# Attention's maxima one to two units ahead of the weights, and unread products around unit 0

## The chip, the cores and the metric

The kernel runs on one core of a Trainium2 chip. A core has five engines with an instruction queue each, and each queue runs in order: PE (TensorE, matrix products into the accumulator memory PSUM), DVE (VectorE), ACT (ScalarE), POOL (GpSimd) and SP (SyncE, which only issues DMAs here). ACT and POOL issue some DMAs too. PEld is PE's loading of the stationary operand. The metric is the device time of one execution in microseconds; lower is better.

## The reference

The input is one sequence `x` of 2048 rows and 448 columns. The output is a gated mix, `g * a + (1 - g) * b`, with `g` the sigmoid of `x` times a vector. `a` is a long convolution along the sequence (its kernel K comes out of a state space model, and both are multiplied in the frequency domain). `b` is attention with a memory:

```python
q = (x @ wq) ... reshape(B, H, N, L, Dh)      # 16 heads of 28, 4 segments of 512 rows; k and v alike
for s in range(N):
    qs, ks, vs = q[:, :, s], k[:, :, s], v[:, :, s]
    logits = jnp.einsum("bhqd,bhkd->bhqk", qs, ks) * scale + mask
    p = _softmax(logits, axis=-1)
    a_dot = jnp.einsum("bhqk,bhkd->bhqd", p, vs)
    ...                                       # a_mem: what the memory of earlier segments gives
    o = g * a_mem + (1.0 - g) * a_dot
...
return o @ wo
```

Inside a segment the mask is causal. The softmax needs the largest logit of each row.

## The kernel before, in words

Up to about 484 us the kernel computes K, transforms `x`, and projects queries, keys and values, which it keeps in device memory. Then `second_half` (L1187) runs, and the change lies wholly in it.

**Units and steps.** Attention is cut into 16 units: unit `i` is segment `i // 4` and one group of four heads. Each piece of work is a Python generator, and `step` (L1193) issues its next part. So the order of PE's instructions is written out by hand in the loops of `second_half`: `k.mm` and `k.tr` (L1351 to L1355) are kept in program order. The other queues are ordered by a planner that follows the readiness it expects; it runs when the kernel is built.

**Maxima, `maxima(i)`, L954 to L987.** Six steps (`MSTEPS`) multiply queries by keys once, in low precision, and take each row's largest logit on DVE (L974, results in `mx`). The steps differ in width: in the first two each product has 512 columns, in the next two 384 and 128, in the last two 256. A seventh step does nothing. The eighth transposes `mx` on PE (L982), copies it with the sign turned on ACT and DVE (L984, L985, both out of the same PSUM bank `ps_m`, of which there is one), and writes it with a DMA from POOL (L986) into a spare row of the unit's queries `qu`. That row meets a row of ones of the keys, so that the products of the weights come out less their maximum.

**Weights, `weigh(i)`, L989 to L1016.** Six steps (`STEPS`) of the same widths in the same order multiply keys by queries, three times for precision, and apply the exponential on ACT (L1005, result in `PT`); POOL then zeroes what the mask hides (L1016). They read all of `qu`, the spare row too, and so wait for L986's DMA to land. Maxima take the heads in the other order, so that a step of maxima and the step of weights behind it lie on other row groups of the array.

**Values, `values(i)`, L1018 to L1037**, multiply `PT` by V. **`seg_end(s)`, L1128**, follows each segment: `norm` (L1074) gathers the sums of the rows by four DMAs from POOL (L1080), inverts them on DVE and sends them through device memory (`inverse`, L1039; its DMAs `RD` and `r`, L1049 and L1050, from POOL too), then products, scalings, the projection by `wo`, and `recall` of the memory for the next segment. `skip` (L1098) has a product on POOL (L1103, `xt`). `divide` (L1140) does the last segment's scaling group by group on PE and DVE, at the places in `DIVIDE`.

**Other work in the rounds.** `cv` is the convolution in the frequency domain (`convolve`, L562; `gk`, `gu`, `pr` in the names), stepped in units 1 to 12. `last` and `join` (L646, L651) end it in units 14 and 15. `turn_over(n)` (L1204) issues `n` products of 512 columns on the whole array, whose result nobody reads (`ps_pv<-wz`).

**The order around the change.** `transform_k` ("K's first step", eight rounds) runs with the steps of unit 0's maxima between its own, and its last two rounds with the first two steps of unit 1's maxima. Four more steps of unit 1's maxima follow, each behind three unread products. Then unit by unit there are six rounds. In each round of unit `i` before the change there come one step of the maxima of unit `i + 2` (`ahead`), one step of the weights of unit `i`, then other work; in rounds 0 and 1 the last two steps of the maxima of unit `i + 1` (`behind`), the transposes among them. PSUM's three large banks `ps_a` serve maxima, weights and convolution by turns. Queries and keys have four buffers each, and `load(i + 3)` is issued at the start of unit `i` from SP.

Of the kernel before, what the change touches and what calls it, by code (L numbers as in the profile page):

```python
# [459 lines left out]
class Feed:  # L460
# [9 lines left out]
    def step(self):  # L470
        tag = next(self.steps, None)
        self.count += 1
        self.done, self.held = tag is None, tag == "pe"
        cost = tag if isinstance(tag, float) else 0.0
        self.ends = cost < 0
        return abs(cost)
# [58 lines left out]
def transform_k(nc, k, fp):  # L535


    k2 = k.kb.rearrange("p b q -> p (b q)")
    gkv = k.GK.rearrange("k r n d -> (k r) n d")
    for i in range(8):  # L540
        gs = fp.tile([128, 4, 4, 112], F32, tag="gs", name="gs", bufs=4)
        pts = [k.ps("a") for jj in range(2)]
        for b in range(2):
            o = (32 * b + 4 * i) * 112
            for j in range(4):
                r = slice(32 * j, 32 * j + 32)
                k.mm(
                    pts[j // 2][:, j % 2, :448], k.s1k[r, b], k2[r, o : o + 448],
                    start=(b == 0), stop=(b == 1), tile_position=(32 * j, 0),
                )  # L550
        for jj in range(2):
            to = gs[:, :, 2 * jj : 2 * jj + 2].rearrange("p n j q -> p j n q")
            pt = pts[jj][:, :, :448].rearrange("p j (n q) -> p j n q", n=4)
            if jj == 0:
                nc.scalar.activation(to, pt, AF.Copy)
            else:
                nc.vector.tensor_copy(to, pt)
        k.mark(k.dma(gkv[:, 4 * i : 4 * i + 4], gs.rearrange("p n j q -> p n (j q)")))
        yield
# [71 lines left out]
def finish(nc, k, fp):  # L631

    bv = k.BB.rearrange("k r (h w) d -> (k r) h w d", h=2)
    ov = k.out.rearrange("(n h w) d -> h n w d", h=2, w=16)
    tv = k.TB.rearrange("(n h w) d -> h n w d", h=2, w=16)
    yv = k.YD.rearrange("(n h w) d -> h n w d", h=2, w=16)
    bts, rest = {}, {}  # L640

    def load(wc):
        bts[wc] = fp.tile([128, 2, 2, D], F32, tag="bt", name="bt", bufs=5)
        k.dma(bts[wc], bv[:, :, 2 * wc : 2 * wc + 2])

    def join(wc):  # L646
        rest[wc] = fp.tile([128, 2, D], F32, tag="rest", name="rest", bufs=6)
        for h in range(2):
            k.dma(rest[wc][64 * h : 64 * h + 64], tv[h, :, 2 * wc : 2 * wc + 2])

    def last(wc):  # L651
        ws = slice(2 * wc, 2 * wc + 2)
        py = k.ps("a")
        for w in range(2):
            for h in range(2):
                k.mm(
                    py[64 * h : 64 * h + 64, w, :D], k.fc, bts[wc][:, h, w],
                    start=True, stop=True, tile_position=(0, 64 * h),
                )
        yo = rest.pop(wc)  # L660
        for w in range(2):
            i = 2 * wc + w
            nc.vector.scalar_tensor_tensor(yo[:, w], py[:, w, :D], k.gt2[:, i : i + 1], yo[:, w], ALU.mult, ALU.add)
        for h in range(2):
            k.dma(yv[h, :, ws], yo[64 * h + 48 : 64 * h + 64])
        for h in range(2):
            k.dma(ov[h, :48, ws], yo[64 * h : 64 * h + 48])

    return load, join, last
# [517 lines left out]
def second_half(nc, k, ap, tp, fp, fin):  # L1187

    none = object()

    def step(g):  # L1193
        return next(g, none) is not none

    nothing = iter(())
    attend(nc, k, ap)
    k.load(0)


    wz = ap.tile([128, SEG], BF16, name="wz")
    nc.gpsimd.memset(wz, 1.0)

    def turn_over(n):  # L1204
        pt = k.ps("pv")
        for _ in range(n):
            k.mm(pt, wz[:, :128], wz, start=True, stop=True)

    first = transform_k(nc, k, tp)
    ms = {i: k.maxima(i) for i in range(16)}  # L1210
    for r in range(8):
        step(first)
        if r == 1:
            k.load(1)
        for _ in range((0, 1, 2, 1, 2, 1, 1, 0)[r]):
            step(ms[0])
        if r >= 6:
            step(ms[1])

    pm = k.ps("m")  # L1220
    k.tr(pm[:16, :128], k.gt, k.ident)
    g16 = ap.tile([16, 128], F32, name="g16")
    nc.vector.tensor_copy(g16, pm[:16, :128])
    k.dma(k.GD.rearrange("(i p) -> i p", p=128), g16)
    k.gt2 = ap.tile([128, 16], F32, name="gt2")
    for h in range(2):
        k.dma(k.gt2[64 * h : 64 * h + 64], k.GD.rearrange("(n h w) -> h n w", h=2, w=16)[h])
    fp = fp()
    cv = convolve(nc, k, fp)
    step(cv)  # L1230
    k.load(2)
    vals = k.values(0)
    step(vals)
    for r in range(4):
        turn_over(3)
        step(ms[1])
    ends = []
    acc = 0.0
    n = 0
    for i in range(16):  # L1240
        k.load(i + 3)
        ahead = ms.get(i + 2, nothing)
        behind = ms.get(i + 1, nothing)
        w = k.weigh(i)
        for r in range(6):
            if r in WARM:
                turn_over(WARM[r])
            step(ahead)
            step(w)
            if r == 0:  # L1250
                step(behind)
            if r == 1:
                if i > 0:
                    step(vals)
                step(behind)
                if i % 4 == 0 and i > 0:
                    ends.append(k.seg_end(i // 4 - 1))
            if r != 1 or i == 13:
                for _ in range(2 if i == 13 else 1):
                    while ends and not step(ends[0]):  # L1260
                        ends.pop(0)
            if (i, r) in DIVIDE:
                k.divide(DIVIDE[i, r])
            if 1 <= i <= 12:
                acc += RATIO
                while acc >= 1.0:
                    acc -= 1.0
                    step(cv)
            if i == 11 and r == 2:
                k.skip_last()  # L1270
            if i == 13 and r < 5:
                load_b(r)
            if i == 14 and r >= 2 or i == 15 and r < 4:
                last(n)
                turn_over(1)
                if n < 2:
                    join(n + 6)
                if n < 3:
                    load_b(n + 5)
                n += 1  # L1280
        step(w)
        if i == 1:
            k.load_wo()
        if i > 0:
            vals = k.values(i)
            step(vals)
        if i == 12:
            for _ in cv:
                pass
            load_b, join, last = finish(nc, k, fin())  # L1290
        if i == 13:
            for wc in range(6):
                join(wc)
    for e in ends:
        for _ in e:
            pass
    k.last_end(step, vals)
# [1 line left out]

RATIO = 1.15  # L1300
WARM = {3: 1, 4: 3, 5: 3}
DIVIDE = {(14, 2): 0, (14, 5): 1, (15, 3): 2}

# [1 line left out]
def gated_mix(ctx, tc, k):  # L1307
# [231 lines left out]
    with ExitStack() as st:  # L1539
        psum_pool(  # L1540
            st,
            {"m": ([128, 512], 1), "a": ([128, 2, 512], 3), "pv": ([128, 512], 1)},
        )
        ap = pool(st, "ap", "right")
        k.mk = ap.tile([128, 512], F32, name="mk")
        nc.sync.dma_start(k.mk, k.c_mk)
        k.dbc = ap.tile([128, D], F32, name="dbc")
        tp, cs = ExitStack(), ExitStack()

        def fourier():  # L1550
            tp.close()
            kst.close()
            return pool(cs, "fp")

        def final():
            cs.close()
            return pool(st, "fin")

        second_half(nc, k, ap, pool(tp, "tp"), fourier, final)
# [34 lines left out]
```

## Time and profile before

| | |
|---|---|
| time, median of 3 runs | 895.89 us (895.46 to 905.81) |
| the profiled execution: its time, its span | 897.03 us, 895.3 us |
| busy: PE, DVE, ACT, POOL | 86%, 67%, 60%, 19% of the span |
| mean granted clock of PE | 0.93 |
| first weights of unit 0, of unit 1, of unit 15 | 518.2, 533.1, 855.2 us |
| instructions | 18968 |

The span runs from the first to the last instruction that the profiler recorded; the execution's own time is 1.7 us longer. A line of a timeline has the start, the duration in us, the engine, the line of the kernel, the operation, the names of what is written and read (`out<-in`), the shape and a count; in brackets stands how long the engine was idle before it and what ended that. A line of the waits has who waited for whom, the total in us, how often, and the longest. A line that cuts the time into stretches has each engine's busy time with its instructions, then PE's granted clock as a share of full speed, the share of the DMA engines' time, and GB/s. Ends of PE's products are modelled, and a wait for several things is put down to the last one.

### The profile page before, as it was taken

To read this page: it belongs to the slowest core of one execution; us is meant where nothing else is said; L and a number is where in the kernel's file an instruction comes from. 1 tells how busy PE (TensorE), PEld (TensorE's weight loads), DVE (VectorE), ACT (ScalarE), POOL (GpSimd) and SP (SyncE) were. 2 spreads that over 40 slices of the span, in tenths; PEclk is the share of its full clock that TensorE was granted. 3 is DMA by queue.
4 is the path that set the end of the run, shared out by engine and by line. 5 is a ranking of instruction groups with operands and counts; after the bars stand their busy time and mean duration, and the time that the engine had idled before them with its cause. 6 is when DMAs were issued, how large, how long until landed. Compare 5 with 4: busy or idle time off the path is not lost.

```text
span 895.3 us, 18968 instructions
## 1 busy us (share of the span) xinstructions
PE 765.6 (86%) x7573; PEld 413.3 (46%) x7573; DVE 602.6 (67%) x1162; ACT 536.8 (60%) x636; POOL 172.7 (19%) x217
## 2 busy tenths in 40 slices
PE   1688597799887998898997989989998999788997
PEld 1365364465544664455653344434443444334433
DVE  7986187758867767688666866656575736665564
ACT  4876388878978788878885235554454434332220
POOL 5222200110011001110110012132313122333110
PEclk9996799999988999969999969999999999989799
DMA  8258662334334334333255995576556565455773
GB/s 240 83 137 270 208 208 62 97 114 140 122 101 137 123 107 130 127 105 111 100 194 204 333 339 177 182 237 212 176 197 202 175 212 193 152 191 205 197 239 101
DMA packets 88290, 153.11 MB, mean 171 GB/s; under 512 B 20626, under 2 KB 57162, under 8 KB 88154
## 3 DMA queue, kind: packets, MB, share of 16 engines
q1 hardware_dynamic: 79130, 140.83, 48.2%
q10 hardware_dynamic: 7424, 9.18, 3.0%
q0 software_dynamic: 1648, 1.89, 0.7%
q8 instruction: 60, 0.98, 0.5%
q14 instruction: 28, 0.23, 0.1%
HBM read 90.87 MB, written 60.63 MB: 169 GB/s over the span
## 4 chain that ended last, share of the span: by engine, by line
PE 57%; DVE 14%; ACT 13%; DMA 7%; issue 5%; POOL 1%; SPq 1%; ACTq 0%; DVEq 0%; POOLq 0%
PE ps_m L1352 22%; PE ps_a L1352 17%; PE ps_pv L1352 7%; PE ps_arg L1352 6%; PE ps_k L1352 4%; ACT cs L1317 4%; DVE jk L974 3%; PE ps_m L1355 2%; DMA dn<-pvs 2%; DVE Y L397 2%; DMA WD<-wsp 2%; ACT L1317 1%; DVE X L393 1%; DVE Y L398 1%; DVE pin_f L211 1%
## 5 line engine op out<-in xcount | busy, mean ns | idle before, releaser
L1005 ACT ACTIVATE PT<-ps_a 128x1024 f32<-128x1024 f32 (+1 forms) x96 | 84.5, 881 | 120.0 <-PE ps_a L1352 114.9
L974 DVE CUSTOM_DVE_ANT_0 jk<-ps_a,mk 128x512 f32<-128x512 f32 (+3 forms) x256 | 125.0, 488 | 43.9 <-PE ps_a L1352 36.6
L359 POOL TENSOR_TENSOR EX<-EX,cab 128x1024 f32<-128x1024 f32 x28 | 54.0, 1929 | 344.2 <-ACT EX L1317 317.4
L1317 ACT ACTIVATE cs<-ps_arg 128x1024 f32<-128x1024 f32 x111 | 107.3, 1019 | 15.7 <-PE ps_arg L1352 13.6
L1352 PE MATMUL ps_m<-xh,w 112*128 112x512 f32 x256 | 95.0, 424 | 10.9 <-DMA w<-WD 9.1
L1352 PE MATMUL ps_a<-qu,ku 32*128 32x512 f32 (+3 forms) x768 | 90.2, 356 | 1.8 <-DVE mx L974 1.1
L1352 PE MATMUL ps_k<-Y,X 128*32 128x64 f32 x3584 | 70.2, 238 | 22.1 <-DVE Y L398 22.1
L393 DVE TENSOR_TENSOR X<-EX,cs 128x1024 f32<-128x1024 f32 x56 | 69.8, 1247 | 26.1 <-ACT cs L1317 23.6
L1352 PEld LDWEIGHTS ps_k<-Y,X 128*32 128x32 f32 x3584 | 60.5, 121 | 51.4 <-DVE Y L398 35.7
L1016 POOL TENSOR_SCALAR_AFFINE_SELECT PT<-PT 128x256 f32<-128x256 f32 (+1 forms) x96 | 47.4, 496 | 173.9 <-ACT PT L1005 173.7
L397 DVE TENSOR_TENSOR Y<-EY,cs 128x1024 f32<-128x1024 f32 x56 | 70.1, 1252 | 0.0
L1352 PEld LDWEIGHTS ps_a<-qu,ku 32*128 32x128 f32 x768 | 62.7, 195 | 10.5 <-issue 3.2
L399 DVE SCALAR_TENSOR_TENSOR Y<-EY,cs 128x512 f32<-128x512 f32 x56 | 40.8, 728 | 38.5 <-ACT cs L1317 37.5
L1352 PEld LDWEIGHTS ps_m<-xh,w 112*128 112x128 f32 x256 | 50.0, 195 | 35.9 <-issue 19.3
L1317 ACT ACTIVATE cs<-cs,bhp 128x1024 f32<-128x1024 f32 x56 | 64.4, 1150 | 1.8
L1317 ACT ACTIVATE EY<-ps_arg 128x1024 f32<-128x1024 f32 x52 | 52.7, 1039 | 10.0 <-PE ps_arg L1352 10.0
L1352 PE MATMUL ps_a<-ku,qu 32*128 32x512 f32 (+3 forms) x256 | 46.6, 397 | 10.8 <-DVE mx L974 7.2
L1352 PE MATMUL ps_m<-xl,w 112*128 112x512 f32 x128 | 51.8, 404 | 0.0
L1352 PEld LDWEIGHTS ps_a<-ku,qu 32*128 32x128 f32 x256 | 22.5, 191 | 58.6 <-DVE mx L974 29.6
L1352 PEld LDWEIGHTS <-lh 64*128 64x128 bf16 x392 | 21.4, 96 | 59.0 <-issue 46.7
L1352 PE MATMUL ps_arg<-ct,lh 64*128 64x512 bf16 x224 | 42.7, 396 | 4.5 <-ACT cs L1317 3.6
L1352 PE MATMUL ps_arg<-ce,lh 64*128 64x512 bf16 x168 | 37.7, 430 | 9.3 <-ACT EY L1317 4.5
(214 smaller groups left out, 1402.8 us busy)
## 6 DMA issues: line engine op xcount, KB each, us to landing
w<-WD SPq DMA_DIRECT2D x32, 448.0 KB, 3.8
qu<-QD SPq DMA_DIRECT2D x16, 512.0 KB, 6.4
ku<-KD SPq DMA_DIRECT2D x16, 512.0 KB, 4.8
GU<-gs SPq DMA_DIRECT2D x32, 224.0 KB, 3.4
GK<-gs SPq DMA_DIRECT2D x8, 896.0 KB, 3.6
gk<-GK SPq DMA_DIRECT2D x32, 224.0 KB, 4.4
gu<-GU SPq DMA_DIRECT2D x32, 224.0 KB, 3.5
BB<-bs ACTq DMA_DIRECT2D x16, 448.0 KB
```

Of the source, the lines that this page charges most:

```text
L211: x = op(*args, **kw)
L359: nc.gpsimd.tensor_tensor(o, o, cab, ALU.mult)
L393: v.tensor_tensor(X, ex, t[:, :, 0], ALU.mult)
L397: v.tensor_tensor(Y[:, :, :, :32], lo, y[:, :, :, ::-1], ALU.mult)
L398: v.tensor_tensor(Y[:, 0, :, 32:], ey[:, :, 32:], y[:, 0], ALU.mult)
L399: v.scalar_tensor_tensor(Y[:, 1, :, 32:], ey[:, :, 32:], -1.0, y[:, 1], ALU.mult, ALU.mult)
L974: v.tensor_tensor_reduce(junk[:, :n], pt[:, x, o : o + n], k.mk[:, SEG - n :], 1.0, -3e38, ALU.add, ALU.max, mx[:, 3 - t, h : h + 1],)
L1005: nc.scalar.activation(PT[:, 2 * hp : 2 * hp + 2, 512 * b : 512 * b + n], pt[:, :, :n], AF.Exp, scale=SCALE)
L1016: nc.gpsimd.affine_select(sl, sl, pat, ALU.is_ge, 0.0, base=0, channel_multiplier=-1)
L1317: x = op(*args, **kw)
L1352: tc.keep_in_program_order(nc.tensor.matmul(*args, **kw))
L1355: tc.keep_in_program_order(nc.tensor.transpose(*args))
```

## The change

The four steps of unit 1's maxima between K's first step and unit 0 are left out, with their twelve unread products. In the rounds, maxima run in another order: rounds 0 to 3 of unit `i` take the third to the sixth step of unit `i + 1`, rounds 4 and 5 the first two steps of unit `i + 2`. The seventh and eighth step of unit `i + 1` (the transposes, the copies and the DMA of L986) come in round 4, behind that round's weights. In unit 0 ten unread products stand in front of round 0's maxima and three in front of each later round's; in the other units they stay as they were (one, three and three in rounds 3, 4 and 5). The end of a segment makes no step in round 4 where it made none in round 1, so that its first step comes in round 1. Two of the three places of `divide` in the last units move.

```diff
     step(vals)
-    for r in range(4):
-        turn_over(3)
-        step(ms[1])
     ends = []
...
         w = k.weigh(i)
         for r in range(6):
-            if r in WARM:
+            if i == 0:
+                turn_over(3 if r else 10)
+            elif r in WARM:
                 turn_over(WARM[r])
-            step(ahead)
+            step(behind if r < 4 else ahead)
             step(w)
-            if r == 0:
+            if r == 4:
+                step(behind)
                 step(behind)
             if r == 1:
                 if i > 0:
                     step(vals)
-                step(behind)
                 if i % 4 == 0 and i > 0:
                     ends.append(k.seg_end(i // 4 - 1))
-            if r != 1 or i == 13:
+            if r != 4 or i == 13:
...
-DIVIDE = {(14, 2): 0, (14, 5): 1, (15, 3): 2}
+DIVIDE = {(14, 4): 0, (15, 0): 1, (15, 3): 2}
```

## The prediction

> **What bounds the kernel now.** I read the page first, for the engines' shares and the chain that ended last.
>
> ```profile
> span 895.3 us, 18968 instructions
> PE 765.6 (86%) x7573; PEld 413.3 (46%) x7573; DVE 602.6 (67%) x1162; ACT 536.8 (60%) x636; POOL 172.7 (19%) x217
> PE 57%; DVE 14%; ACT 13%; DMA 7%; issue 5%; POOL 1%; SPq 1%; ACTq 0%; DVEq 0%; POOLq 0%
> ```
>
> TensorE (PE) is the bound on average. The edit touches only the stretch from K's first step to the end, so I cut that stretch: first the front of the units, then units 0 and 1. The columns are the busy time of each engine, the granted clock, the DMA share and GB/s.
>
> ```profile
> 509.70:518.10 8.40, 5.11 (x27) 2.09 (x28) 7.55 (x30) 0.11 (x1) 0.00 (x0) 1.00 0.93 331
> 518.10:533.10 15.00, 14.26 (x79) 8.35 (x79) 8.63 (x35) 5.79 (x7) 2.91 (x7) 0.55 0.90 331
> 533.10:548.80 15.70, 15.70 (x133) 7.42 (x133) 10.57 (x35) 9.01 (x11) 3.59 (x8) 1.00 0.43 142
> ```
>
> Three different limits stand side by side. In front of unit 0 PE is idle for 3.3 of 8.4 us. Unit 0 runs its 15 us at a clock of 0.55, with 79 matmuls where unit 1 has 133. Unit 1 has PE busy for the whole of its 15.7 us at full clock: there, whatever PE must wait for is added to the time. PE's waits from unit 0 on, and the timeline of PE in front of unit 0, say what the idle time is:
>
> ```profile
> PE ps_a L1352 <- DVE mx L974: 8.2, 10, 2.5
> PE ps_a L1352 <- DVE pr L599: 7.0, 8, 4.4
> PE ps_a L1352 <- DMA ku<-KD: 3.3, 1, 3.3
> ```
>
> ```profile
> 510.30 0.81 PE L1352 MATMUL ps_pv<-wz 128*128 128x512 bf16 x3
> 518.12 0.79 PE L1352 MATMUL ps_a<-ku,qu 32*128 32x512 f32 x2 [3.26 <-DMA ku<-KD]
> ```
>
> PE's queue is in order. The maxima of unit 2 stand in front of the first weights of unit 0, and they wait for unit 2's keys until 518.12; the weights of unit 0 need none of them.
>
> **The chain that the change moves.** A unit's maxima must come back as rows of `qu` before its weights: four transposes, a copy on ACT, one on DVE, a DMA from POOL, its landing. Unit 1's pass, in the timeline of all engines, and two answers on the landing of that DMA (first in the window 500 to 535, two of them; then all 16):
>
> ```profile
> 522.02 1.01 PE L1355 MATMUL ps_m<-ident,mx 128*4 128x128 f32 x4
> 523.07 0.59 ACT L984 ACTIVATE mn<-ps_m 4x512 fp32r<-4x512 f32 x1
> 523.69 0.68 DVE L985 SCALAR_TENSOR_TENSOR mn<-ps_m,mn 4x512 fp32r<-4x512 f32 x1 [1.72 <-ACT mn L984]
> 524.66 0.58 POOL L986 DMA_DIRECT2D qu<-mn  x1 [1.03 <-DVE mn L985]
> ```
>
> ```profile
> DMA to landing us min/median/max: 3.2/4.2/5.2
> DMA to landing us min/median/max: 2.2/3.2/5.3
> ```
>
> From the first transpose to POOL's issue it is 2.64 us here, of which the transposes take 1.01 at half clock. On PE at full clock they take about half, so 2.2 us. With the landing the chain takes 4.4 us at best, 5.4 us at the median landing of 3.2, and 7.5 at the longest. Before, it starts in round 1 and has five rounds. After, it starts in round 4, behind that round's weights, and is needed at the first product of the next unit: one round and a bit. The wait itself is not new, but its cover is.
>
> **Part 1: the front.** Four maxima steps and 12 unread products leave the stretch before unit 0. Ten products stand in round 0 instead: 10 x 0.27 (0.81 for three) from 510.30 ends at 513.0. Unit 1's next maxima have their data, and they share PE with weights on other row groups, as the rows of the next fence show, so the first weights start near 513.1 and not at 518.2. The landing of unit 0's own maxima doesn't hold them; POOL's timeline has its DMA out early, and 508.65 + 3.2 is 511.9:
>
> ```profile
> 508.65 0.61 POOL L986 DMA_DIRECT2D qu<-mn  x1 [25.92 <-DVE mn L985]
> ```
>
> That is -5.1 us at the start of unit 0. The products are all on PE's path; in rounds 1 to 5 there are 15 of them, 4.1 us, where seven stood. Unit 0 at full clock, by rows of unit 1 in part 2 (weights 0.96 us for 512 columns, in four rounds, and 0.62 for 256, in two): 5.1 for the weights, 4.1 for the products, 0.6 for the transposes, and an estimated 1.8 for waits on DVE: 11.6 us instead of 14.9. So PE would stand at the first weights of unit 1 at 524.7, where it stood at 533.1.
>
> It won't go on there. The transposes fall near 522.5 (524.7 less one round of products and weights, 1.5, and the transposes, 0.6). DMA is full there:
>
> ```profile
> 525.00:530.00 5.00, 4.93 (x28) 3.11 (x27) 2.80 (x15) 1.93 (x2) 1.04 (x3) 0.50 1.03 385
> ```
>
> so I take the long landing of this window: 2.2 + 5.2 = 7.4, unit 1's weights at 529.9, a gain of 3.2 us (bounds: chain 4.4, gain 6.2; chain 7.8 with cold transposes, gain 2.8).
>
> **The clock after that wait.** PE then is idle from 524.7 to 529.9. What follows idle time of that length is seen in unit 11, behind the longest wait of PE for `pr`, 4.4 us:
>
> ```profile
> 766.00:768.00 2.00, 0.80 (x2) 0.29 (x4) 2.00 (x6) 0.00 (x0) 0.00 (x0) 0.80 0.63 229
> 768.00:770.00 2.00, 2.00 (x8) 0.47 (x4) 1.42 (x7) 0.00 (x0) 0.00 (x0) 0.50 0.62 170
> 770.00:772.00 2.00, 2.00 (x15) 0.86 (x15) 0.34 (x1) 1.02 (x2) 0.00 (x0) 0.85 0.79 233
> ```
>
> Together (0.20 + 0.50 + 0.15) x 2 / 0.5 = 3.4 us at half clock, in a stage with convolution matmuls like unit 1's: +1.7 us on a unit that PE bounds. Unit 0 of before is the far row: there the clock stayed low for 0.45 x 15 / 0.5 = 13.5 us after 3.3 us of idleness, with PE 95% busy, and that would be +6.7. I take 1.7, since unit 1 is of unit 11's kind; the lower bound is 0. The Trainium skill, "TensorE: Matmul & The Clock Gate", Part 1, says that an idle window of about 3.4 us halves the clock and that about 3.4 us of sustained work restores it. The drop agrees with unit 0's row (0.55 behind the gap); the quick return doesn't agree with it, only with unit 11's. By the page the term is 1.7 at most, by unit 0's row 6.7, which would make the sum 5.0 us larger.
>
> **Part 2: the later units.** Between round 4's weights and the next unit's first weights PE has, in unit 1:
>
> ```profile
> 545.00 0.62 PE L1352 MATMUL ps_a<-qu,ku 32*128 32x256 f32 x6
> 545.55 1.02 PE L1352 MATMUL ps_a<-gu,cf 64*128 64x448 f32 x4
> ...
> 548.77 0.50 PE L1352 MATMUL ps_a<-ku,qu 32*128 32x512 f32 x2
> 548.78 0.96 PE L1352 MATMUL ps_a<-qu,ku 32*128 32x512 f32 x6
> ```
>
> 545.62 to 548.78, 3.16 us. Maxima and weights start together (548.77, 548.78), so wider maxima in round 5 cost PE nothing: weights cover them. The transposes come to this stretch, 0.6, so 3.76 us cover a chain of 5.4: PE waits 1.6 us at the start of unit 2. The same for units 2, 11 and 12:
>
> ```profile
> 562.37 0.62 PE L1352 MATMUL ps_a<-qu,ku 32*128 32x256 f32 x6
> 566.86 0.97 PE L1352 MATMUL ps_a<-qu,ku 32*128 32x512 f32 x6
> ...
> 771.24 0.62 PE L1352 MATMUL ps_a<-qu,ku 32*128 32x256 f32 x6
> 775.02 0.96 PE L1352 MATMUL ps_a<-qu,ku 32*128 32x512 f32 x6
> ...
> 790.70 0.79 PE L1352 MATMUL ps_a<-qu,ku 32*128 32x256 f32 x6
> 794.84 0.96 PE L1352 MATMUL ps_a<-qu,ku 32*128 32x512 f32 x6
> ```
>
> Pauses of 3.87, 3.16 and 3.35, with 0.6 each: waits of 0.9, 1.65 and 1.45. With unit 1 that makes 5.6 us. Units 3, 4, 6, 10 and 13 get 1.0 each, between these, an estimate: 5.0. Units 5, 7, 8, 9 and 14 have a segment's end or last products in that stretch and I take them as covered. Together 10.6. While PE waits, DVE and ACT empty their queues, so some of the 8.2 us that PE waits for `mx` later goes; I take 3 off: +7.6. Bounds: chain 4.4, some 2.5 us before the same relief; chain 6.4, about 20.
>
> **Part 3: the segment's end** starts one round sooner and skips round 4, so that POOL's queue holds its DMAs in front of the moved one. In unit 4, POOL's timeline, and PE's for round 4's weights:
>
> ```profile
> 592.01 2.04 POOL L1080 DMA_DIRECT2D dn<-pvs  x4 [1.71 <-ACT pvs L1036]
> 599.50 0.75 POOL L1049 DMA_DIRECT2D RD<-rs  x1 [4.41 <-DVE rs L1047]
> 602.24 0.53 POOL L1050 DMA_DIRECT2D r<-RD  x1 [1.99 <-DMA RD<-rs]
> ```
>
> ```profile
> 601.01 0.61 PE L1352 MATMUL ps_a<-qu,ku 32*128 32x256 f32 x6
> ```
>
> This is paced by data (values, then a landing, then a reciprocal), not by the round, and it is out of the queue at 602.8, before the moved DMA could be ready (601.6 + 2.2 = 603.8). I put it at 0, between a small gain and the rival below.
>
> **Part 4: the end.** Unit 14 gets four steps of maxima more, beside its weights on PE; `divide` moves behind them. I take 0, with 2 us either way. The moved loads, `vals` and SP's order stay as they are.
>
> **The sum**, against the profiled execution: -3.2 + 1.7 + 7.6 = +6.1, so 897.0 becomes 903.1. That execution lies 1.1 above the median of 895.9; on the median's scale it is 902.
>
> **Rivals.** (1) The chain is covered, and the result is faster. It decides at a chain of about 4.4 us: POOL's DMA landing in 2.2, its least. For it: the maxima ahead of round 4 are the narrow ones. Against it: the median landing is 3.2. Front -6.2, no drop of the clock, later waits 2.5 that the 8.2 us absorb almost wholly: 897.0 - 6.2 + 0.5, on the median's scale 890. (2) POOL's queue holds the moved DMA, behind a tensor product that itself waits for a load:
>
> ```profile
> POOL xt L1103 <- DMA xt<-in_A_u: 17.9, 4, 7.3
> ```
>
> Such a wait of up to 7.3 us was covered by rounds; now it would reach PE at two or three units, and the clock falls behind each: 902 + 2 x 7 = 916. Against it: the products come in the rounds around the unit's start, not in round 4. (3) The edit moves nothing: unit 1 can't start before the full DMA queue is through, near 530 to 533, and the later waits are absorbed: 896. The quoted stretch 525 to 530 with its DMA share of 1.03 speaks for it; that PE waited for a load just once, for unit 2's keys, speaks against it.
>
> **How the numbers follow.** My forecast, 0.52; rival 1, 0.25; rival 2, 0.11; rival 3, 0.12. A measurement of this kernel tells about 2%, 18 us, from no change. The forecast and rivals 1 and 3 lie inside it. Faster by more needs both of rival 1's gains and relief in every unit: 0.03. Slower by more is rival 2 and the forecast's upper tail (chain 6.4): 0.11. The range takes in rival 1 and stops short of rival 2's centre: 889 to 915. The forecast's own range is 896 to 911.
>
> **What would show it.** Right: the first weights near 513, full clock through unit 0, PE idle for some 5 us before unit 1's weights with the DMA of `mn` landing last, and idle times of 1 to 2 us in front of units 2, 3, 4, 12 and 13. Wrong: no idle time there and landings of about 2.2 us (rival 1); `xt` or `RD` in front of `mn` on POOL (rival 2); unit 1 starting at 533 (rival 3).

## The result and the profile after

The changed kernel takes 922.96 us (median of 4 runs, 921.36 to 925.24), the kernel before 896.54 on the same chip (895.46 to 905.81). The ratio is 1.0273, with an interval of 1.0212 to 1.0333: slower, and above the range that was forecast (the ratio is taken over the single runs, not from the two medians). Ratios here, and the medians of the kernel before in the experiments, leave out executions in the chip's slower state. The profiled execution took 921.36 us, 24.3 more than that of before. In the code of after the line numbers of the helpers are one smaller (`k.mm` records as L1351 and `k.tr` as L1354).

The page of after: the span, the busy time of each engine, and the share of each engine in the chain that ended last.

```profile
span 919.6 us, 18963 instructions
...
PE 775.2 (84%) x7562; PEld 419.4 (46%) x7579; DVE 601.2 (65%) x1162; ACT 537.0 (58%) x636; POOL 173.4 (19%) x217
...
PE 53%; DMA 13%; DVE 12%; ACT 12%; issue 7%; POOL 2%; SPq 1%; DVEq 0%; ACTq 0%; POOLq 0%
```

PE has 9.6 us more busy time than before, and a smaller share of the span. Its work hardly grew: the loads of stationary operands (PEld) are six more, since 25 unread products stand around unit 0 where 19 stood. (PE's own count is lower by 11 only because records of products are missing: it falls short of the loads.) In the chain, PE's share fell from 57% to 53% while that of the DMAs rose from 7% to 13%. So two things happened at once: PE waits for transfers, and its products take longer.

To separate the two I cut both traces at the first weights of unit 1, behind which the work is nearly the same (by the loads, ten products more in after, all of them maxima). The columns are those of the prediction: busy time of PE, PEld, DVE, ACT and POOL, the granted clock, the DMA share, GB/s. First after, then before:

```profile
524.65:919.60 394.95, 347.67 (x2210) 157.60 (x2225) 221.30 (x591) 146.68 (x180) 86.23 (x144) 0.91 0.56 180
```

```profile
533.07:895.30 362.23, 330.24 (x2215) 147.02 (x2215) 218.54 (x575) 146.44 (x180) 85.87 (x145) 0.96 0.59 192
```

This stretch is 32.7 us longer. PE is idle for 47.3 us of it (394.95 - 347.67) where it was idle for 32.0: +15.3. The other 17.4 us are busy time, for ten products more. The clock says why: half-clock time is twice the missing share. With the clocks before rounding, 0.910 and 0.955, that is 71 us after and 33 before; 38 us more at half speed make at most 19 us of busy time.

In front of that cut the change gains. From the first transposes of unit 0 (506.43 before, 503.61 after, which the edit doesn't reach) to the first weights of unit 1 it was 26.64 us and is now 21.04: -5.6. The transposes themselves come 2.8 us sooner in this execution, in front of all that was edited. The balance is -2.8 - 5.6 + 32.7 = +24.3 us, the difference of the two executions.

What PE waits for, from 505 us to the end of after (total, times, longest), and then the landing of L986's DMA, by the view of that line:

```profile
PE ps_a L1351 <- DMA qu<-mn: 15.9, 11, 4.1
PE ps_a L1351 <- DVE mx L974: 10.3, 12, 4.5
```

```profile
DMA to landing us min/median/max: 2.3/4.0/6.1
```

Before has no wait of the first kind: PE now waits for the maxima's DMA at the start of eleven units. The wait for `mx` did not fall (8.4 before, in the same stretch). The median landing grew from 3.2 to 4.0 us. Unit 1's pass, in the timeline of all engines of after:

```profile
518.24 0.60 PE L1354 MATMUL ps_m<-ident,mx 128*4 128x128 f32 x4
518.88 0.59 ACT L984 ACTIVATE mn<-ps_m 4x512 fp32r<-4x512 f32 x1
519.58 0.67 DVE L985 SCALAR_TENSOR_TENSOR mn<-ps_m,mn 4x512 fp32r<-4x512 f32 x1
520.55 0.58 POOL L986 DMA_DIRECT2D qu<-mn  x1 [0.89 <-DVE mn L985]
...
524.65 0.79 PE L1351 MATMUL ps_a<-qu,ku 32*128 32x512 f32 x2 [4.07 <-DMA qu<-mn]
```

From the first transpose to the issue it is 2.31 us, and 4.1 more to the weights. Nothing stood between `mn` and its DMA on POOL.

**The clock behind such a wait** is seen best in unit 7, since in before that unit had PE busy all the time at full clock. The whole unit, before and after:

```profile
656.04:674.16 18.12, 18.12 (x148) 8.25 (x146) 12.61 (x38) 9.94 (x12) 3.95 (x8) 1.00 0.60 200
```

```profile
662.77:685.50 22.73, 22.46 (x144) 10.14 (x146) 10.78 (x29) 9.22 (x12) 3.47 (x7) 0.79 0.34 101
```

PE is busy for all but 0.3 us of it, with as many loads (146), and yet it takes 4.6 us longer. PE's timeline of after has the wait in front of it:

```profile
662.77 0.79 PE L1351 MATMUL ps_a<-qu,ku 32*128 32x512 f32 x2 [2.68 <-DMA qu<-mn]
```

The granted clock changes at the points of a fixed grid only: in each trace of this case all its changes lie a whole number of 3.41 us apart. Stretches cut at this grid show the clock in steps, around the start of unit 7 and then of unit 5, whose wait was about as long (2.58 us, until 606.16):

```profile
658.77:662.18 3.41, 1.01 (x8) 0.30 (x4) 3.06 (x13) 0.92 (x1) 0.01 (x1) 1.00 0.93 348
662.18:665.59 3.41, 2.82 (x9) 1.71 (x11) 0.71 (x1) 1.02 (x1) 0.00 (x0) 0.50 0.34 132
665.59:669.01 3.42, 3.42 (x18) 1.05 (x18) 2.29 (x7) 0.74 (x1) 0.41 (x1) 0.50 0.26 67
669.01:672.42 3.41, 3.41 (x32) 1.18 (x24) 0.47 (x4) 0.29 (x1) 0.41 (x1) 0.50 0.00 0
672.42:675.83 3.41, 3.40 (x34) 1.72 (x26) 0.87 (x4) 1.68 (x3) 0.00 (x0) 1.00 0.12 23
```

```profile
604.15:607.57 3.42, 1.41 (x9) 0.92 (x11) 1.94 (x8) 0.34 (x1) 0.00 (x0) 1.00 0.89 329
607.57:610.98 3.41, 3.41 (x16) 1.17 (x14) 0.76 (x3) 1.35 (x2) 0.41 (x1) 0.50 0.04 10
610.98:614.39 3.41, 3.41 (x43) 1.45 (x39) 1.85 (x9) 1.79 (x3) 0.41 (x1) 1.00 0.37 135
```

In unit 7 the clock is at half for three steps, from 662.18 to 672.42, although PE has no pause behind 662.77. The wait cost 2.7 us and the slow products behind it 4.6. Unit 5 has one step at half clock. Unit 1 is like unit 7: 4.07 us of waiting, half clock for three steps from 522.23 to 532.47, a unit of 20.9 us where it had 15.7.

### The profile page after: what moved, and what is told of

The parts are those of the page before. It is cut to its first block, busy times and chain, and to the rows that moved or that the text cites. A ratio compares the mean times of both kernels' runs of the same rounds, so it can differ in the third digit from the quotient of the medians.

```text
span 919.6 us, 18963 instructions
## 1 busy us (share of the span) xinstructions
PE 775.2 (84%) x7562; PEld 419.4 (46%) x7579; DVE 601.2 (65%) x1162; ACT 537.0 (58%) x636; POOL 173.4 (19%) x217
## 4 chain that ended last, share of the span: by engine, by line
PE 53%; DMA 13%; DVE 12%; ACT 12%; issue 7%; POOL 2%; SPq 1%; DVEq 0%; ACTq 0%; POOLq 0%
PE ps_m L1351 19%; PE ps_a L1351 16%; PE ps_pv L1351 6%; PE ps_arg L1351 6%; DMA qu<-mn 4%; PE ps_k L1351 4%; ACT cs L1316 4%; DVE jk L974 2%; DVE Y L397 2%; PE ps_m L1354 2%; ACT L1316 2%; DMA WD<-wsp 1%; DMA xt<-in_A_u 1%; DMA RD<-rs 1%; DMA dn<-pvs 1%
## 5 line engine op out<-in xcount | busy, mean ns | idle before, releaser
L1351 PE MATMUL ps_a<-qu,ku 32*128 32x512 f32 (+3 forms) x768 | 93.1, 361 | 18.4 <-DMA qu<-mn 15.9
L1351 PE MATMUL ps_m<-xh,w 112*128 112x512 f32 x256 | 93.8, 419 | 9.3 <-DMA w<-WD 7.5
L1351 PE MATMUL ps_k<-Y,X 128*32 128x64 f32 x3584 | 70.4, 238 | 22.3 <-DVE Y L398 22.3
L1351 PEld LDWEIGHTS ps_k<-Y,X 128*32 128x32 f32 x3584 | 60.6, 122 | 51.6 <-DVE Y L398 36.5
L1351 PEld LDWEIGHTS ps_a<-qu,ku 32*128 32x128 f32 x768 | 64.2, 197 | 26.5 <-issue 9.9
L1351 PEld LDWEIGHTS ps_m<-xh,w 112*128 112x128 f32 x256 | 49.1, 192 | 34.1 <-issue 17.7
L1351 PE MATMUL ps_a<-ku,qu 32*128 32x512 f32 (+3 forms) x256 | 47.4, 407 | 11.1 <-DVE mx L974 8.2
L1351 PE MATMUL ps_m<-xl,w 112*128 112x512 f32 x128 | 51.1, 399 | 0.0
L1351 PEld LDWEIGHTS ps_a<-ku,qu 32*128 32x128 f32 x256 | 23.5, 199 | 59.0 <-issue 28.5
L599 DVE TENSOR_TENSOR pr<-ps_a,ks 128x896 f32<-128x896 f32 x32 | 34.8, 1086 | 20.8 <-PE ps_a L1351 16.4
L1351 PEld LDWEIGHTS <-lh 64*128 64x128 bf16 x392 | 21.3, 96 | 59.0 <-issue 46.3
L1351 PE MATMUL ps_arg<-ct,lh 64*128 64x512 bf16 x224 | 42.3, 393 | 4.5 <-ACT cs L1316 3.6
```

Source lines behind the costliest of these rows:

```text
L599: nc.vector.tensor_tensor(pr[c], pt, ks.pop(c), ALU.mult)
L1351: tc.keep_in_program_order(nc.tensor.matmul(*args, **kw))
```

## The experiments

The expectations call two theories A and B. A: what costs is the wait for the landed maxima at each unit's start, and the clock behind it. B: what costs is the new order of the maxima themselves, which steps share PE, DVE and the PSUM banks with which other work. Ratios are to the kernel before on the same chip; and the median of before was 903.18, 897.03 and 905.72 us beside the three groups of runs (e1 to e4, e5 to e8, e9 to e12).

**e3_no_wait: the same instructions, and no wait.** L986's DMA goes to device memory that nobody reads, so PE has nothing to wait for; the spare row is not written, and the exponentials are taken without their maxima.

```diff
-        k.pdma(q.rearrange("(j e) i q -> e j i q", e=32)[28].bitcast(F32), mn.bitcast(F32))
+        spare = k.dr.tile([4, 2, SEG], F32, tag="sp", name="spare", bufs=2)
+        k.pdma(spare, mn.bitcast(F32))
```

> The changed kernel, but the DMA of mn writes to device memory that nobody reads, so that the weights don't wait for it and the exponentials are taken without their maxima; the chain's own work all stays. Theory A: the whole loss of the later units (some 30 us) goes, 888 to 896. Rival B (order of the steps, banks) and rival C (the segment's end one round sooner): the time stays over 910. In between: the difference to 890 is what the order costs.

Measured: 900.69 us (10 runs), ratio 0.9981 (0.9945 to 1.0017). The whole loss is gone. Its profiled execution was one of the longer ones (908.9 us), so I read lengths of single units in it, not the total. From the first transposes to the first weights of unit 1 it takes 18.0 us, 8.6 less than before. Units 2 to 8 are back within 0.7 us of their lengths of before (unit 7: 18.3 us, where after had 22.7). Unit 0 in the windows, and then PE's largest wait:

```profile
517.92:529.80 11.88, 10.49 (x88) 5.98 (x89) 8.49 (x33) 5.81 (x7) 3.38 (x7) 1.00 1.01 350
```

```profile
PE ps_a L1352 <- DVE mx L974: 12.2, 15, 4.3
```

Unit 0 takes 11.9 us at full clock and unit 1 follows without a wait for the DMA (1.1 us for `mx`). The loss of the changed kernel hangs on the wait: theory A. But a front that is 8.6 us shorter gave nothing in the median, so the rest of the change gives about that much back elsewhere. In this execution unit 1 is 3.6 us longer than before (19.3 us, at half clock from 531.07 to 537.89), and the larger wait for `mx` (12.2 us, before 8.4) and the later `divide` (below) are 5 us.

**e7_chain_r5: more of the suspected wait.** The transposes and the DMA come one round later, so their cover shrinks to the next unit's first maxima.

```diff
-            if r == 4:
+            if r == 5:
                 step(behind)
                 step(behind)
...
-            if r != 4 or i == 13:
+            if r != 5 or i == 13:
```

> The changed kernel with the transposes, copies and the DMA of mn in round 5 instead of round 4, behind that round's weights; the segment's end makes no step in round 5. Theory A: each unit's wait grows by the round that is left out, 2 to 3 us in some 14 units, and the clock falls behind nearly all of them: waits for mn's DMA of 45 to 60 us where there were 15.9, and 955 to 980 in all. If the place of the chain isn't what costs: 915 to 930.

Measured: 1002.55 us, one run; more than expected. The waits, and the windows from unit 0 on:

```profile
PE ps_a L1351 <- DMA qu<-mn: 69.9, 15, 6.9
```

```profile
516.48:1000.80 484.32, 378.71 (x2294) 169.69 (x2308) 231.72 (x632) 153.13 (x187) 88.75 (x151) 0.85 0.49 157
```

The waits for the DMA grew by 54 us over after, and the stretch from unit 0 on by 74 (484.32, after 409.85). Of these 20.5 are busy time (378.71, after 358.17), at a clock of 0.85. So each us of waiting cost about 1.4 us in all. That is A's price list with a second amount: the wait, and four tenths of it again in slower products. (Unit 0 itself starts 6.7 us later than in after.)

**e1_chain_r2: the wait taken away by an earlier start.** Rounds 0 and 1 each do two steps of unit `i + 1`'s maxima, so the transposes come in round 2 and have four rounds of cover.

```diff
-            step(behind if r < 4 else ahead)
+            if r < 2:
+                step(behind)
+            elif r > 3:
+                step(ahead)
             step(w)
-            if r == 4:
+            if r < 2:
+                step(behind)
+            if r == 2:
                 step(behind)
                 step(behind)
...
-            if r != 4 or i == 13:
+            if r != 2 or i == 13:
```

> The changed kernel with the four steps of unit i+1's maxima made two a round in rounds 0 and 1 (one ahead of the weights, one behind), and the transposes, copies and the DMA of mn in round 2 instead of round 4; the segment's end makes no step in round 2. All else, the front too, is the changed kernel's. Theory A (the landing of mn's DMA comes too late at each unit's start, and the idle time of PE also halves its clock): the waits of PE for mn's DMA fall from 15.9 us to under 1, the half-clock time behind unit 0's start falls from 72 us to about 45 as before the change, and the front's gain of some 6 us stays: 888 to 896. Rival B (the new order of maxima beside weights costs, through the PSUM banks and VectorE): still over 910, since the maxima lie even closer together.

Measured: 940.23 us, ratio 1.0413 (1.0364 to 1.0463): slower still, against what A expected. The waits, and the windows from unit 0 to the end:

```profile
PE ps_a L1356 <- DVE mx L974: 17.4, 21, 2.4
...
PE ps_a L1356 <- ACT PT L1005: 5.5, 5, 3.5
```

```profile
513.19:936.70 423.51, 374.19 (x2297) 172.03 (x2312) 233.97 (x632) 152.06 (x187) 88.30 (x151) 0.89 0.56 180
```

No wait for the maxima's DMA is left, as intended. In its place PE waits for the reduction of the maxima on DVE (17.4 us, 21 times) and for the exponentials, and the clock is the lowest but for e7. That two steps of maxima in one round need the three banks twice would explain it; it was not tested by itself. This is B's mechanism. It holds for this order; that it isn't the changed kernel's is what e3 shows, where that order is kept and the loss goes.

**e6_chain_r2_even: the same cover, evenly spread.** Two steps of unit 1's maxima return to the front, so that each round has one step and the transposes come in round 2.

```diff
+    for r in range(2):
+        turn_over(3)
+        step(ms[1])
...
-                turn_over(3 if r else 10)
+                turn_over(3 if r else 4)
...
-            step(behind if r < 4 else ahead)
+            step(behind if r < 2 else ahead)
             step(w)
-            if r == 4:
+            if r == 2:
...
-            if r != 4 or i == 13:
+            if r != 2 or i == 13:
```

> The changed kernel with the maxima two steps further ahead and one step a round as before: two more steps of unit 1's maxima stand before unit 0 (with six products), rounds 0 and 1 take the last two steps of unit i+1, its transposes, copies and DMA come in round 2, and rounds 2 to 5 take the first four steps of unit i+2. The segment's end makes no step in round 2. Theory A (the late landing and the clock behind it): no wait for mn's DMA, half-clock time at 45 to 55 us, and the time within 1% of the kernel before. Then the loss of the run with two steps a round in rounds 0 and 1 came from their crowding on VectorE and the banks, not from the chain. Rival B (any order but the old one costs): 910 or more although nothing waits for the DMA.

Measured: 912.36 us, ratio 1.0149 (1.0026 to 1.0272).

```profile
PE ps_a L1354 <- DVE mx L974: 14.9, 16, 3.7
...
PE ps_a L1354 <- DMA qu<-mn: 3.2, 1, 3.2
```

The waits for the DMA are down to one, in unit 1; those for `mx` are 14.9 us. The result lies between the theories: without the DMA's waits this order still pays for `mx`, which the order of before (8.4 us) did better. The interval is too wide to say how much of the loss is left.

**e2_fill_r0 and e11_fill_r0_4: work in the wait.** Eight (or four) unread products between the maxima and the weights of round 0, in every unit from 1 on.

```diff
             step(behind if r < 4 else ahead)
+            if r == 0 and i > 0:
+                turn_over(8)
             step(w)
```

> The changed kernel with eight unread products (2.2 us at full clock) between the first maxima and the first weights of each unit from 1 on, where PE waits for the DMA of mn. Theory A, with the clock as the larger part: PE isn't idle there, half-clock time falls from 72 us to about 50, and the time falls by 5 to 10 us, to 913 to 918, although 120 products are added. If the wait alone is the cost and the clock is incidental: units whose wait was short get the products on top, 923 to 935. Rival B: 15 x 2.2 us on top, 945 or more.

> The changed kernel with four unread products (1.1 us at full clock) between the first maxima and the first weights of each unit from 1 on; with eight it was 918 us, with half-clock time down from 72 to 32 us. If the clock is the larger part of the loss: nearly as little half-clock time with half of the products, and 912 to 917, under both the changed kernel and the run with eight. If products help only as long as PE would wait anyway: 918 to 923.

Measured: with eight 918.19 us, ratio 1.0167 (1.0117 to 1.0217); with four 916.87, ratio 1.0155 (1.0076 to 1.0234). The trace of e2, its waits and the windows from unit 1's weights:

```profile
PE ps_a L1353 <- DMA qu<-mn: 5.0, 4, 2.3
```

```profile
525.85:915.20 389.35, 353.81 (x2312) 161.50 (x2337) 221.49 (x591) 146.78 (x180) 86.36 (x144) 0.96 0.58 183
```

By the loads 112 products more were issued than in after (2337 and 2225), and the stretch is no longer (389.35 us against 394.95). The granted clock is 0.96 instead of 0.91: with full-array products in the gap the clock stays up. The time of the filler replaces the time of the wait and of the slow clock. As a gain this is not established, because of the next run.

**e12_changed_again: the changed kernel once more**, unedited, on the chip of e9 to e11.

> The changed kernel as it is, on the chip of the three runs beside it, to compare them with: 919 to 925 us if the chips agree; the waits for mn's DMA 13 to 18 us.

Measured: 920.26 us (914.46 to 925.8), ratio 1.0172 (1.0097 to 1.0246). PE's waits for the DMA are 14.1 us (15.9 in the first trace), those for `mx` 6.6 (10.3). So the size of the loss is known to about 1.0 to 3.3%, and runs with ratios of 1.015 to 1.025 can't be told from the changed kernel.

**e4_front_only and e5_front_held: the front alone.** On the kernel before, unit 0 leaves out the maxima of unit 2 in round 0, so that its first weights need not wait for unit 2's keys, and does two steps in round 5. e5 also puts three unread products in each of unit 0's rounds, 18 where seven stood: the first four changed lines of the diff are e5's alone, the others stand in both.

```diff
         for r in range(6):
-            if r in WARM:
+            if i == 0:
+                turn_over(3)
+            elif r in WARM:
                 turn_over(WARM[r])
-            step(ahead)
+            if i > 0 or r > 0:
+                step(ahead)
             step(w)
+            if i == 0 and r == 5:
+                step(ahead)
```

> The kernel before with one edit: in unit 0 the maxima of unit 2 begin in round 1 and end with two steps in round 5, so that unit 0's first weights don't stand behind the wait for unit 2's keys. No unread products are added and every chain stays five rounds ahead. If the front's gain comes from that wait and from the clock behind it: first weights 3 us sooner, part of unit 0 at full clock, 889 to 894. If unit 1 is bound by the full DMA queues in any case: 895 to 898.

> The kernel before with unit 0 alone changed: its first weights don't stand behind unit 2's maxima (these come in rounds 1 to 5, two steps in round 5), and three unread products stand in each of its rounds, 18 where seven stood. All chains stay five rounds ahead. In the run without the products the clock was at half for 20 us from 519 on and nothing was gained. If the products hold the clock: unit 0 takes 12 to 13 us instead of 15, first weights of unit 1 at about 527, and the time is 4 to 6 us under the kernel before. If they don't: as that run, no difference.

Measured: e4 899.30 us, ratio 0.9968 (0.9927 to 1.0009); e5 897.75, ratio 0.9998 (0.996 to 1.0036). No difference in either. In e4 unit 0 starts sooner and then runs at half clock for some 20 us. In e5 unit 0 holds its clock, takes 14.0 us, and the first weights of unit 1 come 23.7 us behind the transposes (before 26.6). The windows of e5 show where the 2.9 us go:

```profile
524.00:526.00 2.00, 0.61 (x8) 0.42 (x8) 1.61 (x10) 0.60 (x1) 0.49 (x2) 1.00 1.02 403
526.00:528.00 2.00, 0.65 (x4) 0.65 (x6) 0.42 (x2) 0.00 (x0) 0.35 (x1) 0.52 1.02 349
528.00:530.00 2.00, 2.00 (x12) 0.86 (x6) 1.40 (x4) 0.84 (x1) 0.00 (x0) 0.50 1.04 394
...
534.00:536.00 2.00, 2.00 (x20) 0.74 (x16) 0.00 (x0) 0.00 (x0) 0.04 (x1) 0.50 0.00 0
536.00:538.00 2.00, 2.00 (x24) 0.75 (x16) 0.13 (x1) 1.08 (x2) 0.00 (x0) 0.92 0.03 8
```

PE pauses, 2.6 us of it for loads of keys (`ku`), while the DMA engines are full (share 1.02), and the half clock that unit 0 had before now lies in unit 1, from 526 to 536, with PE wholly busy from 528 on. Unit 1 takes 19.6 us instead of 15.7. The front's gain alone is therefore worth nothing here.

**e8_mn_by_act: another queue for the DMA.** ACT issues L986's DMA.

```diff
-        k.pdma(q.rearrange("(j e) i q -> e j i q", e=32)[28].bitcast(F32), mn.bitcast(F32))
+        k.adma(q.rearrange("(j e) i q -> e j i q", e=32)[28].bitcast(F32), mn.bitcast(F32))
```

> The changed kernel with the DMA of mn issued by ACT instead of POOL, and nothing else changed. Theory A: what counts is when it lands. If ACT's DMAs land sooner than POOL's median of 4.0 us in this kernel, by a microsecond or two, the waits for it fall from 15.9 us to some 4 to 8 and the time to 905 to 915. If ACT's queue, behind its exponentials and copies, issues it later than POOL did, the waits grow and the time is 923 to 935.

Measured: 920.26 us, ratio 1.0266 (1.0168 to 1.0363). No gain. Its waits, the view of L986, and unit 1 in the timeline of ACT and PE:

```profile
PE ps_a L1351 <- DMA qu<-mn: 13.2, 4, 9.5
```

```profile
L986 ACTq EVENT_SEMAPHORE  x15: 17/17/5111, 507.8 to 872.9; - x15
```

```profile
527.61 0.57 ACTq L986 DMA_DIRECT2D qu<-mn  x1
528.23 0.60 ACT L1005 ACTIVATE PT<-ps_a 128x512 f32<-128x512 f32 x1 [5.19 <-DMA gk<-GK]
...
533.62 0.79 PE L1351 MATMUL ps_a<-qu,ku 32*128 32x512 f32 x2 [9.48 <-DMA qu<-mn]
```

`mn` was complete at 523.82, and its DMA left ACT at 527.61. The longest of L986's own waits in ACT's queue took 5.1 us (least, median and longest are 17, 17 and 5111 ns), until a load of the convolution (`gk`) had landed, and the exponential behind it stood for 5.2. Why this DMA waits for that load the trace doesn't say. PE waited 9.5 us for its landing, in unit 1 alone. The other units waited 3.7 us in all, where after has 11.8, yet the time at half clock is not lower (75 us from unit 0 on, after 72, without each trace's last stretch). Five steps of it, 17 us, lie behind unit 1's wait (525.95 to 543.02). What lowers the clock in the later units of this run I have not found.

**e9_load_late: loads out of the way?** `load(i + 3)` is called behind the weights of round 1, to see if the 1 MB of queries and keys lengthens the landing.

```diff
     for i in range(16):
-        k.load(i + 3)
...
             step(w)
+            if r == 1:
+                k.load(i + 3)
```

> The changed kernel with the load of unit i+3's queries and keys (two DMAs of 512 KB) called for in round 1 of unit i, behind the weights, instead of ahead of the unit. In the changed kernel's trace these loads leave SP within a microsecond of mn's DMA at the end of the unit before, and its landing takes 4.0 us in the median. If they are what makes the landing long: the median landing falls to 2.5 to 3.2, the waits for it from 15.9 to 5 to 9 us, the clock follows, and the time is 908 to 916. If the landing is long for other reasons: 920 to 926.

Measured: 920.75 us, ratio 1.0195 (1.013 to 1.026).

```profile
DMA to landing us min/median/max: 2.1/3.5/5.9
```

Inconclusive. The planner put SP's loads at nearly the same times as before the edit (in unit 4 queries are issued at 602.2 in after and at 602.0 here), so the landing was not tested without them. What makes it long stays open.

**e10_old_ends: the places of before for the segment's end and `divide`.**

```diff
-            if r != 4 or i == 13:
+            if r != 1 or i == 13:
...
-DIVIDE = {(14, 4): 0, (15, 0): 1, (15, 3): 2}
+DIVIDE = {(14, 2): 0, (14, 5): 1, (15, 3): 2}
```

> The changed kernel with two of its places put back: the segment's end skips round 1 and not round 4, and divide stands at its old places in units 14 and 15. If these places cost what the later units lost in their end (unit 15 is longer by 1.1 us in each run with the new places, units 13 and 14 by 2 to 3): 2 to 5 us less than the changed kernel. Theory A alone: within 2 us of the changed kernel, and unit 15 at its old length.

Measured: 926.34 us, ratio 1.0248 (1.018 to 1.0317). No gain. Unit 15 is back from 41.2 to 40.1 us, as in every run with the old places of `divide`; the new places cost 1.1 us. The waits:

```profile
PE ps_a L1351 <- DMA qu<-mn: 9.4, 6, 3.9
PE ps_m L1351 <- DVE mn L985: 7.3, 5, 1.5
```

With the old places PE waits less for the DMA, and more in front of products that need the one bank `ps_m` while `mn` is read from it (7.3 us, after 2.8). The places are not the cause of the loss.

None of these kernels beats the one before. The best are e4 and e5, equal to it.

## Why the prediction missed the size

**Mechanism and sign: right.** The forecast was a loss in which the landing of L986's DMA gates the starts of the units. After shows eleven such waits, and e3 shows that without them the loss is gone.

**Part 1, the front: -3.2 predicted, -5.6 measured.** From the transposes of unit 0 to its first weights it takes 6.1 us instead of 11.8, the -5.1 of the prediction within 0.6. Unit 0 needs 10.8 us of work at a clock of 0.92 (11.6 predicted). The chain to unit 1's weights is 6.4 us (518.24 to 524.65), not 7.4, and so the wait is 4.07 where 5.2 was predicted. This part erred by being too cautious. In another way it was too hopeful: in e5 a front shorter by 2.9 us is followed by a unit 1 that is 3.9 us longer.

**"The clock after that wait": +1.7 predicted, +17.4 measured. This is the step that failed.** It went wrong twice. The prediction charged the clock to one wait, unit 1's, and charged nothing for the waits of 1 to 2 us in "Part 2". And it took unit 11's row, 3.4 us at half clock, as the near one. That is one step of the clock's grid, the least there is. Units 7 and 1 show three steps, 10.2 us, behind waits of 2.68 and 4.07 us. The far row, unit 0 of before with 13.5 us, was nearer to both. Unit 11 of after again has one step (a wait of 1.27 us, then 3.4 us at half clock), so both kinds exist in one kernel, and the prediction had both rows before it and priced only one. How many steps a wait brings is in part luck. In e12, the same kernel, unit 5 has three steps behind a wait of 2.63 us, where the first trace has one behind 2.58; the grid's next point comes 0.4 us behind the wait there, and 1.4 us in the first trace. The Trainium skill, "TensorE: Matmul & The Clock Gate", Part 1, gives about 3.4 us of sustained work for the return to full clock. Unit 11's one step agrees with that, and the step of unit 7 that was wholly busy and brought nothing back (665.59 to 669.01) doesn't. Here the measurement decides.

**Part 2, the later units: +7.6 predicted, +15.3 measured.** PE's waits for the DMA from unit 2 on are 15.9 - 4.07 = 11.8 us, close to the 10.6 before relief. Where they lie was predicted badly. The starts of units 2, 3, 12 and 13, forecast at 0.9 to 1.65, have 0.69, 0.21, 0.45 and 1.06 us. Those of units 5 and 7, forecast at 1.0, have 2.58 and 2.68, and that of unit 9, forecast as covered, has 2.06. So the near agreement of the totals is partly luck. The median landing was 4.0 us, not the 3.2 that was carried over from before. And the chain was longer than 2.3 us, its length in most units, where other work stood in front of it: from the first transpose to the issue it took 6.1 us for unit 9 and 4.7 for unit 13, both behind a segment's end, and 3.9 for unit 11. For unit 9, whose transposes start at 697.85:

```profile
699.16 0.55 DVE L1045 RECIPROCAL rc<-dn 128x64 f32<-128x64 f32 x1 [3.27 <-DMA dn<-pvs]
702.46 0.67 DVE L985 SCALAR_TENSOR_TENSOR mn<-ps_m,mn 4x512 fp32r<-4x512 f32 x1
702.85 0.53 POOL L1050 DMA_DIRECT2D r<-RD  x1 [1.17 <-DMA RD<-rs]
703.97 0.60 POOL L986 DMA_DIRECT2D qu<-mn  x1
```

DVE stood 3.27 us for the segment's end and then had its reciprocal, a product of the convolution and two maxima in front of `mn`. The prediction took the segment's end in unit 8 as cover only. With a chain of 2.3 us and the same landings the waits of units 9, 11 and 13 would not be there (an estimate: 3.8, 1.5 and 2.4 us sooner, against waits of 2.06, 1.27 and 1.06). The relief of 3 us did not come in this trace: from unit 1 on the waits for `mx` rose by 1.6 us (8.2 to 9.8), though in e12 they are 6.6. With 11.8 and 1.6 the term is 13.4 of the 15.3.

**Part 3, the segment's end, 0: right in the time**, by e10, where the old places gain nothing. Not in the chain: it delays those of units 9 and 13, at the old places too (3.5 and 5.2 us in e10). **Part 4, the end, 0 with 2 us either way: low.** `divide` costs 1.1 us, and units 13 and 14 are 2.2 and 2.6 us longer; the latter two were not taken apart by a run.

**The sum**: the three terms came out at -5.6, +17.4 and +15.3, against -3.2, +1.7 and +7.6. Of the 21.0 us between the two sums the clock is 15.7 and the waits are 7.7, less 2.4 by the front.

**The rivals.** Rival 1 (covered chain) needed landings of 2.2 us; the median is 4.0. Rival 2 (POOL's queue) had a price of 7 us for each such unit, which unit 7 alone comes near (2.7 and 4.6), but the wrong place: nothing stood in front of `mn` on POOL in unit 1, and in units 9 and 13 its sign, the DMAs of the segment's end, held `mn` there for no more than 0.9 us. Rival 3 (nothing moves) fell with the front's 5.6 us, though e4 and e5 show that its result would have been right for the front alone.

**What stays open**: what a step must hold to bring the full clock back. In all fourteen traces, from 505 us on, 185 steps at half clock had PE busy for 97% or more, and 128 of them led back to full clock: all 98 that held less than four products of 32 or 8 rows, but only 8 of the 44 that held ten or more. So products of few rows seem to count for less. That is a reading of the traces and was not tested by a run of its own; that full-array products in the gap keep the clock (e2) points the same way. Open too are the time at half clock in e8's later units, and what makes the landing long.

## What to carry to other kernels

Where PE bounds a kernel, a wait in its queue has two prices: its own length and the clock behind it. Take the second from the worst row of the trace, in whole steps of the clock, for every wait that is added and not only for the longest; here it was as large as the waits themselves. Before a look-ahead is shortened, add up the whole chain to the landing of its DMA, with the landing as it is under the load of that stretch and with what else stands in the queues of its engines, and ask for slack over the longest landing, not the median. And a gain in a front that ends in a full DMA queue is no gain until the work behind it can start: here the slow clock just moved on by one unit.

## What was unexpected of the hardware

The granted clock moved in steps of 3.41 us on one grid through each trace. From 505 us on, all 55 steps at full clock in which PE was busy for less than 40% were followed by half clock, and none of the 1008 with 90% or more; so a pause need not fill a step: unit 11's was 1.27 us. And a step without a pause did not always bring the clock back: unit 7 was wholly busy at 0.50 from 665.59 to 672.42, and e5 from 528 to 536. In e2, with eight products of the whole array in each unit's gap, the mean clock from unit 1 on was 0.96 where it was 0.91, and 112 products more took no more time.

L986's DMA, of the same 16 KB each time (4 rows of 2 x 512 values of 4 bytes), took 2.3 to 6.1 us to land within one kernel. And issued from ACT it waited 5.1 us, in one unit, for the landing of another load, and held up the exponential behind it (e8).
